# A fused retention and gated feed-forward kernel: 256-token blocks, two tokens a partition, and nine equal tiles

## The chip, the cores and the metric

The kernel runs on one core of one Trainium2 chip. A core has five engines with a queue of instructions each: TensorE (PE in the profile; its weight loads are shown apart as PEld), VectorE (DVE), ScalarE (ACT), GpSimd (POOL) and SyncE (SP), which here only issues transfers. An engine runs its own queue in order and waits for others through semaphores. Transfers run on 16 DMA engines. TensorE reads from SBUF and writes PSUM, which has eight banks of 2 KB a partition.

The metric is the device time of one execution in microseconds. Three runs of the kernel before gave 299.54, 298.88 and 304.79 us, median 299.54.

## What is computed

The reference has two parts. The first is a retention layer: attention without softmax, with a decay by head. The second is a feed-forward layer with `h * cos(h)` between two matrix products.

```python
def _attn_ref(q, k, v):                    # each (8, 8, 576, 64): batch, heads, tokens, head size
    scale = 1.0 / np.sqrt(D_)
    scores = scale * np.matmul(q, k.transpose(0, 1, 3, 2))
    gamma = 1.0 - 2.0 ** (-5.0 - np.arange(H))
    rel = pos[:, None] - pos[None, :]
    Dmat = np.where(rel >= 0, gamma[:, None, None] ** rel[None, :, :], 0.0)
    return np.matmul(scores * Dmat, v)

def _moe_ref(x, w_in, w_out):              # x (4608, 512), w_in (512, 2048), w_out (2048, 512)
    h = x @ w_in
    g = h * np.cos(h)
    return g @ w_out
```

The attention's output, with the heads side by side, is `x`: 8 x 576 = 4608 rows of 512. Inputs and output are float32.

## The kernel before

**Attention.** The 4608 tokens are taken in 36 groups of 128. A batch entry has 576 tokens, that is four and a half groups, so every ninth group is mixed: its second half begins a new entry. For one group:

- `load` (L105) fetches q, k and v, tokens on partitions, with one piece of 64 floats (256 bytes) for each token and head. It is issued from SP.
- `prep` (L131) multiplies q and k by powers of the head's decay (`scaled`, L139) and rounds to bf16, and rounds v. This is on POOL, 1.05 us for q, 1.05 to 1.14 us for k and 0.65 us for v. The powers (`gq`, `gk`) are made at the start from token positions.
- `transposes` (L163) turns q and k so that the head size lies on partitions: on TensorE for groups 0 to 5, and from group 6 by a transposing DMA from SP (L166).
- `scores` (L186) makes k times q for the eight heads, and VectorE multiplies the result by a triangular mask (L206).
- `state` (L218) and `states` (L247) keep the sum of k times v over the tokens of the entry so far. VectorE adds (L286), and a copy in bf16 follows (L277).
- `attn_out` (L292) adds the masked scores times v (`own`, L332) and q times the state (`carried`, L318), and ScalarE or VectorE copies the sum to `xT` (L349).

**Feed-forward.** Rows are taken in tiles; the widths are `[512, 256, 256] + [512] * 7`. `mm1` (L353) makes `h` in blocks of 1024 columns of a two-bank PSUM tile, ScalarE takes the cosine (L372), and VectorE multiplies (L373, `gT`). The first three tiles (rows 0 to 1023) use `mm2` (L375): 16 matmuls of 512 columns for each 128 rows. The other seven tiles use `mm2_seven` (L505), a form of Strassen's method: the product of two 2 x 2 block matrices is made from seven block products (`product`, L467) instead of eight, of 16 matmuls with 256 columns each. It needs sums of quarters of `gT` (`g_sum`, L420; `gs7` is on POOL, the others on VectorE), sums of quarters of `w_out` (`w_sums`, L403) and sums of the results (L515, VectorE).

**Order.** The kernel writes out the order of each engine's queue by hand. The matmuls of the attention of later rows are put between those of the feed-forward of earlier rows: at positions in the lists `todo` for the first tiles, and ahead of some of the seven products (`at`, L820 to L829) for the others. `feed` (L577) is called at each store and issues the next loads, preps and transposes. PSUM banks are named by tags: `a`, `b` and `m` are pairs of banks, `n` and `st` single ones. A new use of a tag waits until the last use has been read out.

**Start.** The first 512 queries come with four tokens a partition (L620), keys and values group by group. TensorE runs 14 matmuls on zeros while they come (L641). The weights come in eight transfers of a quarter of a matrix, cast to bf16, issued from POOL between the first preps; the load of group 4 waits for the sixth of them (L704).

Of the kernel before, what the change touches and what calls it, by code (L numbers as in the profile page):

```python
# [8 lines left out]
F32 = mybir.dt.float32  # L9
# [8 lines left out]
def kernel(  # L18
# [9 lines left out]

# [4 lines left out]
    HG = H // 2  # L39
    DM, DF = moe_w_in.shape  # L40
# [3 lines left out]
    NG = NTOK // P  # L44
    PER = 2 * S // P
    MIX = PER // 2
    HP = P // 2
# [3 lines left out]
    ET = DF // P  # L51

    widths = [512, 256, 256] + [512] * 7
    assert sum(widths) == NTOK
    starts = [sum(widths[:n]) for n in range(len(widths))]
    N_PE_T = 6
    S7 = 3
    LD = 5

    consts = ctx.enter_context(tc.tile_pool(name="consts", bufs=1))  # L60
    first = ctx.enter_context(tc.tile_pool(name="first", bufs=1))
    ld = ctx.enter_context(tc.tile_pool(name="ld", bufs=LD))
    nat = ctx.enter_context(tc.tile_pool(name="nat", bufs=8))
    trp = ctx.enter_context(tc.tile_pool(name="trp", bufs=8))
    retp = ctx.enter_context(tc.tile_pool(name="retp", bufs=4))
# [4 lines left out]
    op = ctx.enter_context(tc.tile_pool(name="op", bufs=2))  # L70
    xp = ctx.enter_context(tc.tile_pool(name="xp", bufs=2))

# [4 lines left out]

    pos_i = consts.tile([P, PER, H], I32)
    pos = consts.tile([P, PER, H], F32)
    lng = consts.tile([P, H], F32)  # L80
    gq = consts.tile([P, PER, H], F32)
    pos_i4 = consts.tile([P, 4, H], I32)
    pos4 = consts.tile([P, 4, H], F32)
    gq4 = consts.tile([P, 4, H], F32)
    gk = consts.tile([P, PER, H], F32)
    ln_scale = consts.tile([P, 1], F32)
    half_pi = consts.tile([P, 1], F32)
    tri = consts.tile([P, P], F32)
    tri_mix = consts.tile([P, P], F32)
    diag2 = consts.tile([P, P], F32)  # L90
    ident = consts.tile([P, P], BF16)
    zeros = consts.tile([P, 512], BF16)
    w_in_sb = consts.tile([P, DG, DF], BF16)
    w_out_sb = consts.tile([P, ET, DM], BF16)

    v_odd = consts.tile([P, 2, H, D], BF16)

    blocks4 = [consts.tile([P, HG, D], BF16, tag=f"sb{x}", name=f"sb{x}") for x in range(4)]

    tiles = {}  # L100
# [4 lines left out]
    def load(g, names="qkv", gate=None):  # L105

        t0 = g * P
        if g % PER == MIX:
            parts = [(0, HP, t0), (HP, P, t0 + HP)]
        else:  # L110
            parts = [(0, P, t0)]
        for name in names:
            src = {"q": q, "k": k, "v": v}[name]
            f = ld.tile([P, H, D], F32, tag="f" + name, name=f"f{name}")
            for p0, p1, t in parts:
                b, s0 = divmod(t, S)
                i = nc.sync.dma_start(  # L117
                    f[p0:p1], src[b, :, s0 : s0 + p1 - p0, :].rearrange("h s d -> s h d")
                )
                if gate is not None:  # L120
                    tc.add_manual_dep(
                        i.ins, gate.ins.name,
                        mybir.DependencyInfo(
                            mybir.DependencyClass.Sync, mybir.DependencyReason.DATA
                        ),
                        reason="weights first",
                    )
                    gate = None
            tiles["f" + name, g] = f

    def prep(g, early=False, kv_first=False):  # L131

        c = g % PER
        fk, fv = (tiles.pop(("f" + n, g)) for n in "kv")
        qks = nat.tile([P, 2, H, D], BF16, tag="qks", name="qks")
        vb = nat.tile([P, H, D], BF16, tag="vb", name="vb")
        qkT = trp.tile([P, 2 * HG, P], BF16, tag="qkT", name="qkT")

        def scaled(eng, m, f, by):  # L139
            eng.tensor_tensor(  # L140
# [8 lines left out]
        if not early and not kv_first:  # L149
            scaled(nc.gpsimd, 0, tiles.pop(("fq", g)), gq)  # L150
# [724 lines left out]
```

## Time and profile before

The profiled execution took 298.52 us, of which 296.8 lie between the first and the last instruction (the span).

| what | value |
|---|---|
| median of three runs, us | 299.54 |
| profiled execution, us | 298.52 |
| its span, us | 296.8 |
| first block of `h` starts, us | 17.95 |
| `h` without a break from, us | 19.73 |
| last addition on VectorE ends; last store issued; span ends, us | 293.35; 294.4; 296.8 |
| DMA bytes | 50.29 MB in 154305 packets |

The largest groups of instructions, as `line engine operation, shape and count | busy us, mean ns | idle time of the engine before them and what ended it`:

```profile
L373 DVE TENSOR_TENSOR gT<-h,cosh 128x1024 bf16<-128x1024 f32 x72 | 88.0, 1222 | 36.4 <-ACT cosh L372 36.3
L372 ACT ACTIVATE cosh<-h,half_pi 128x1024 f32<-128x1024 f32 x72 | 80.2, 1113 | 66.7 <-PE h L364 66.7
L140 POOL TENSOR_TENSOR qks<-fq,gq 128x512 bf16<-128x512 f32 x32 | 33.6, 1052 | 60.8 <-DMA fq<-in_q_dram 56.4
L206 DVE TENSOR_TENSOR ret<-sc,tri 128x1024 bf16<-128x1024 f32 x32 | 38.1, 1218 | 2.8 <-PE sc L194 2.7
```

In the chain of waits, which is followed back from the last instruction, TensorE has 80% of the span, DMA 8% and VectorE 6%. The mean duration of a matmul in the groups is longer than the distance from one start to the next, since matmuls overlap in the array; prices of matmuls are therefore read from a run of them, its length over its count. POOL's line 140 is idle for 56.4 us in all until its query loads arrive; the engine's idle time is no loss where nobody waits for it.

### The profile page before, as it was taken

What the parts mean: (1) busy time and instruction counts of PE and PEld (TensorE: products, weight loads), DVE (VectorE), ACT (ScalarE), POOL (GpSimd) and SP (SyncE); (2) the same over time, 40 slices, a digit from 0 to 9 for tenths busy, and PEclk for the clock granted to TensorE, in tenths of its full rate; (3) what the DMA queues carried; (4) which work ended last, traced back from release to release, by engine and by line L of the source; (5) the groups of instructions that cost most, each with busy time, mean ns of one, the idle gap of its engine ahead of it and who ended that gap; (6) DMA issues with size and microseconds to landing.
All of it is one profiled execution on the core that took longest, in us unless ns stands there. A gap on an engine that the chain in (4) does not pass through costs nothing.

```text
span 296.8 us, 7293 instructions
## 1 busy us (share of the span) xinstructions
PE 285.0 (96%) x3083; PEld 195.9 (66%) x3105; DVE 215.4 (73%) x265; ACT 133.9 (45%) x163; POOL 133.7 (45%) x147
## 2 busy tenths in 40 slices
PE   8899999999999999999999899999999999999994
PEld 3478646858568886457745685488448844884584
DVE  5677718564668996797969856996699669935943
ACT  2656432605246534652456344644464346425620
POOL 2750056445444484683675962389139013101410
PEclk9999999999999999999999999999999999999999
DMA  8999999999999999999999999998950340111013
GB/s 205 213 208 207 211 200 209 201 228 219 220 177 213 203 234 215 208 286 167 185 205 243 231 202 225 198 219 214 225 95 5 95 120 0 38 59 49 0 38 107
DMA packets 154305, 50.29 MB, mean 169 GB/s; under 512 B 140832, under 2 KB 153248, under 8 KB 154272
## 3 DMA queue, kind: packets, MB, share of 16 engines
q1 hardware_dynamic: 149504, 45.10, 77.6%
q0 software_dynamic: 4224, 4.19, 8.5%
q8 instruction: 24, 0.39, 0.6%
q10 hardware_dynamic: 544, 0.52, 0.5%
q14 instruction: 9, 0.07, 0.1%
HBM read 36.70 MB, written 9.44 MB: 155 GB/s over the span
## 4 chain that ended last, share of the span: by engine, by line
PE 80%; DMA 8%; DVE 6%; SPq 2%; issue 1%; ACT 1%; POOL 0%; DVEq 0%
PE h L364 39%; PE o L495 26%; PE o L381 7%; DMA qkT<-qks 4%; DMA fk<-in_k_dram 2%; DMA w_in_sb<-in_moe_w_in_dram 2%; PE sc L194 2%; PE ov L332 2%; DVE gT L373 2%; PE ov L318 2%; DVE gs L437 1%; SPq L117 1%; PE st L265 1%; DVE ot L515 1%; DVE ret L206 1%
## 5 line engine op out<-in xcount | busy, mean ns | idle before, releaser
L364 PE MATMUL h<-xT,w_in_sb 128*128 128x512 bf16 (+2 forms) x820 | 126.8, 313 | 1.5 <-DVE xT L349 0.7
L373 DVE TENSOR_TENSOR gT<-h,cosh 128x1024 bf16<-128x1024 f32 x72 | 88.0, 1222 | 36.4 <-ACT cosh L372 36.3
L372 ACT ACTIVATE cosh<-h,half_pi 128x1024 f32<-128x1024 f32 x72 | 80.2, 1113 | 66.7 <-PE h L364 66.7
L364 PEld LDWEIGHTS <-w_in_sb 128*128 128x128 bf16 x832 | 75.9, 98 | 49.9 <-issue 1.0
L437 POOL TENSOR_TENSOR gs<-gT 128x512 bf16<-128x512 bf16 x24 | 30.6, 1282 | 69.0 <-DVE gT L373 69.0
L140 POOL TENSOR_TENSOR qks<-fq,gq 128x512 bf16<-128x512 f32 x32 | 33.6, 1052 | 60.8 <-DMA fq<-in_q_dram 56.4
L495 PEld LDWEIGHTS <-gs 128*128 128x128 bf16 x456 | 43.1, 98 | 5.8
L140 POOL TENSOR_TENSOR qks<-fk,gk 128x512 bf16<-128x512 f32 x35 | 39.8, 1138 | 9.4 <-DMA fk<-in_k_dram 8.3
L206 DVE TENSOR_TENSOR ret<-sc,tri 128x1024 bf16<-128x1024 f32 x32 | 38.1, 1218 | 2.8 <-PE sc L194 2.7
L495 PEld LDWEIGHTS <-gT 128*128 128x128 bf16 x336 | 32.4, 98 | 6.5 <-DVE gT L373 1.1
L519 ACT COPY ot<-o 128x512 f32<-128x512 f32 x28 | 16.4, 585 | 43.2 <-PE o L495 43.2
L515 DVE TENSOR_TENSOR ot<-ot,o 128x512 f32<-128x512 f32 x34 | 22.6, 683 | 11.9 <-ACT ot L519 7.9
L381 PE MATMUL o<-w_out_sb,gT 128*128 128x512 bf16 x120 | 28.9, 380 | 0.5 <-issue 0.2
L495 PE MATMUL o<-w_out_sb,gT 128*128 128x256 bf16 x224 | 26.6, 273 | 0.6 <-DVE gT L373 0.5
L495 PE MATMUL o<-ws,gs 128*128 128x256 bf16 x224 | 26.8, 273 | 0.0
L495 PE MATMUL o<-w_out_sb,gs 128*128 128x256 bf16 (+1 forms) x232 | 26.8, 269 | 0.0
L155 POOL CAST vb<-fv 128x512 bf16<-128x512 f32 x32 | 20.9, 652 | 8.6 <-DMA fv<-in_v_dram 8.0
L349 ACT CAST xT<-ov 128x1024 bf16<-128x1024 f32 (+1 forms) x18 | 16.5, 917 | 14.2 <-PE ov L318 12.1
L381 PEld LDWEIGHTS <-gT 128*128 128x128 bf16 x128 | 11.8, 98 | 12.5
L437 DVE TENSOR_TENSOR gs<-gT 128x512 bf16<-128x512 bf16 (+1 forms) x22 | 14.6, 664 | 0.4
L495 PE MATMUL o<-ws,gT 128*128 128x256 bf16 x112 | 13.4, 273 | 0.0
L194 PEld LDWEIGHTS <-qkT 64*64 64x64 bf16 (+1 forms) x512 | 8.9, 105 | 6.5 <-ACT qkT L176 2.3
(69 smaller groups left out, 175.4 us busy)
## 6 DMA issues: line engine op xcount, KB each, us to landing
out_dram<-ot SPq DMA_DIRECT2D x35, 256.0 KB, 3.5
fk<-in_k_dram SPq DMA_DIRECT2D x32, 256.0 KB, 5.0
fv<-in_v_dram SPq DMA_DIRECT2D x32, 256.0 KB, 5.2
fq<-in_q_dram SPq DMA_DIRECT2D x30, 256.0 KB, 4.7
w_in_sb<-in_moe_w_in_dram POOLq DMA_DIRECT2D x4, 512.0 KB, 9.5
w_out_sb<-in_moe_w_out_dram POOLq DMA_DIRECT2D x4, 512.0 KB, 16.7
fq<-in_q_dram SPq DMA_DIRECT2D x8, 128.0 KB, 3.7
fk<-in_k_dram SPq DMA_DIRECT2D x8, 128.0 KB, 4.5
```

Source lines behind the costliest of these rows:

```text
L140: eng.tensor_tensor(out=qks[:, m].rearrange("p (b a) d -> p a b d", a=2), in0=f.rearrange("p (a b) d -> p a b d", a=2), in1=by[:, c, :].re ...
L155: nc.gpsimd.tensor_copy(vb, fv)
L206: nc.vector.tensor_tensor(out=ret.rearrange("p a b i -> p (a b) i"), in0=ps.rearrange("p a b i -> p (a b) i"), in1=mask.unsqueeze(1).to_br ...
L349: evac(tiles["x", n][:, :, t0 : t0 + len(gs) * P], ps.rearrange("p c x i -> p c (x i)"))
L364: nc.tensor.matmul(ps[:, j, :], lhsT=w_in_sb[:, dg, (et + j) * P : (et + j + 1) * P], rhs=xT[:, dg, c0 : c0 + w], start=(dg == 0), stop=(d ...
L372: nc.scalar.activation(cosh, ps, ACTF.Sin, bias=half_pi, scale=1.0)
L373: nc.vector.tensor_mul(gT[:, et : et + m, c0 : c0 + w], ps, cosh)
L381: nc.tensor.matmul(ps, lhsT=gT[:, et, tsi * P : (tsi + 1) * P], rhs=w_out_sb[:, et, :], start=(et == 0), stop=(et == ET - 1),)
L437: eng.tensor_tensor(out=tiles["gs", n, x][:, e : e + step], in0=a[:, e : e + step], in1=b[:, e : e + step], op=op_,)
L495: nc.tensor.matmul(dst[i], lhsT=lhs[:, e, j * P : (j + 1) * P], rhs=rhs[:, e, c0:c1], start=(fresh and e == 0 and (i == 0 or len(parts) > 2)),
L515: return lambda: nc.vector.tensor_tensor(out=out_, in0=in0, in1=in1, op=ALU.add)
L519: nc.scalar.copy(t, tiles["all", x])
```

## The change

The kernel function is written anew around the same arithmetic.

- Tokens come in 18 blocks of 256. Queries have two tokens a partition (pieces of 512 bytes) in all blocks, keys and values in the first four (`NP_B = 4`, "pair" blocks); later keys and values keep 256-byte pieces. A block is two chunks of 128 tokens.
- In a pair block a chunk lies on 64 partitions, two tokens deep (`y`). Scores, states and outputs go over `y`; the outputs of a chunk need twice as many matmuls with half the rows, with a drain of TensorE between two halves of them. The columns of `xT` are now even tokens first, then odd ones, so each store is split in two, one for each half of the partitions (`stored_rows`).
- Blocks 0 to 3 are transposed on TensorE, the others by one transposing DMA per block (twice the columns, half the count).
- There are nine tiles of 512 rows. Tile 0 uses 512-column matmuls, now with all four row groups side by side; the eight others use the seven products. Seven of ten tiles did before.
- The loads of block 2 wait for the fifth weight transfer, and the sixth to eighth are issued on POOL between the scalings of block 2; the loads of block 3 wait for the seventh.
- Scalings and transposes of later blocks are issued by `steps_to` at fixed places: after blocks of `h` in tile 1, then at stores.
- `w_sums(7)` moves to POOL. The result buffers `ot` go from two of each tag to one.

```diff
-    widths = [512, 256, 256] + [512] * 7
+    W = 512
+    NT = NTOK // W
+    BK = 256
+    NP_B = 4
+    AHEAD = 3
...
+    def load(j, names="qkv", gate=None):
+        for name in names:
+            src = {"q": q, "k": k, "v": v}[name]
+            if name == "q" or j < NP_B:
+                f = ld.tile([P, H, 2, D], F32, tag="f" + name, name=f"f{name}")
+                for p0, p1, t in parts_of(j * BK, BK, 2):
+                    b, s0 = divmod(t, S)
+                    i = nc.sync.dma_start(
+                        f[p0:p1].rearrange("p h r d -> p h (r d)"),
+                        src[b, :, s0 : s0 + 2 * (p1 - p0), :].rearrange(
+                            "h (p r) d -> p h (r d)", r=2
+                        ),
+                    )
...
+    def scores_y(j, y, banks):
+        pss = [psum.tile([P, HG, P], F32, tag=t, name="sc") for t in banks]
...
+        for he in range(2):
+            nc.vector.tensor_tensor(
+                out=ret[:, he, :, y, :],
+                in0=pss[he],
+                in1=mask[:, y].unsqueeze(1).to_broadcast([P, HG, P]),
+                op=ALU.mult,
+            )
...
+            for swap in (1, 0):
+                for hg in range(0, HG, 2):
+                    for c in chunks[j]:
+                        he = c.k ^ swap
+                        for y in range(2):
+                            for h in (head(he, hg), head(he, hg + 1)):
+                                one(c, h, y, ret[c.rows, he, h % HG, y, :])
+                if swap:
+                    nc.tensor.drain()
...
+    def stored_rows(r0, c0, c1, t):
+        rows = out[r0 : r0 + P * t.shape[1], c0:c1].rearrange(
+            "(j i r) c -> r i j c", r=2, i=HP
+        )
+        for r in range(2):
+            nc.sync.dma_start(rows[r], t[r * HP : (r + 1) * HP])
...
+    def step():
+        nonlocal prepared
+        if prepared < NB:
+            prep(prepared)
+            transpose_dma(prepared)
+            round_v(prepared)
+            prepared += 1
+            load_next()
...
+    w_dma += [load_w_in(e) for e in (1024, 1536)] + [load_w_out(0)]
...
+    load_next(names="kqv", gate=w_dma[4])
...
+    for name in "kq":
+        for y in range(2):
+            scaled(nc.gpsimd, 2, name, y)
+        w_dma += [load_w_out(4 + "kq".index(name) * 4)]
+    round_v(2)
+    w_dma += [load_w_out(12)]
+    load_next(names="kqv", gate=w_dma[6])
...
+    blocks_of = {
+        0: [(et, h * BK, BK) for et in range(0, ET, 4) for h in range(2)],
+        1: [(et, 0, BK) for et in range(0, ET, 4)] + [(et, BK, BK) for et in (0, 8, 4, 12)],
+    }
...
+    def block2_scores():
+        masks = scores(2, "ab")
+        masks[0]()
+        add = sums_of(2, "a")
+        masks[1]()
+        add()()
...
+                (0, 0): {2: lambda: outputs(1, "a", act, vec)},
+                (1, 1): {1: lambda: scores_y(3, 0, ("n", "st"))},
+                (1, 2): {1: lambda: scores_y(3, 1, ("n", "st"))},
+                (1, 3): {2: block3_sums},
...
+            if (n, i) == (1, 1):
+                steps_to(5)
+            if (n, i) == (1, 3):
+                outputs(3, "b", act, vec)
+                for e in range(0, E2, 2):
+                    w_sums(7, e, e + 2)
+            if (n, i) == (1, 5):
+                steps_to(6)
...
+        if n in (1, 2):
+            at = {6: only_intro, 5: mid_unit, 3: end_unit}
+        else:
+            at = {2: first_unit, 5: second_unit} if n < last else {}
+
+        def stored(u):
+            if n == 1:
+                steps_to({3: 7}.get(u, 0))
+            elif n == 2:
+                steps_to({0: 8, 1: 9, 2: 10, 3: 11}[u])
+            else:
+                steps_to({0: 2 * n + 6, 1: 2 * n + 7}.get(u, 0))
```

In this diff an `intro` is the states and scores of a block with their masks, `outputs` the outputs of a block and their copy to `xT`; `only_intro`, `mid_unit`, `end_unit`, `first_unit` and `second_unit` put one of each ahead of the product that they are listed under. The seven products run in the order 1, 2, 6, 4, 7, 5, 3.

## The prediction

> **What bounds the kernel now.** I read the page's first two parts, then TensorE's timeline, then the chain of waits, and last the timelines of the engines that feed TensorE. From the page:
>
> ```profile
> PE 285.0 (96%) x3083; PEld 195.9 (66%) x3105; DVE 215.4 (73%) x265; ACT 133.9 (45%) x163; POOL 133.7 (45%) x147
> ...
> PEclk9999999999999999999999999999999999999999
> DMA  8999999999999999999999999998950340111013
> ```
>
> The clock is full and TensorE is never idle for a whole slice. The DMA engines are busy until about 222 us, which matters only where TensorE waits for them. Its timeline (start, length, what, idle before it) says how often:
>
> ```profile
> 67.53 7.15 PE L364 MATMUL h<-xT,w_in_sb 128*128 128x256 bf16 x64 [0.69 <-DVE xT L349]
> ...
> 82.80 0.42 PE L194 MATMUL sc<-qkT 64*64 64x128 bf16 x16 [0.53 <-DMA qkT<-qks]
> ...
> 166.60 0.42 PE L194 MATMUL sc<-qkT 64*64 64x128 bf16 x16 [1.34 <-DMA qkT<-qks]
> ```
>
> All such gaps between 19.7 and 292.6 us come to about 4.0 us. So the span is a start-up of 19.7, then 272.9 of nearly unbroken matmuls, then a tail of 4.2. Fewer or faster loads cannot give much by themselves; a change wins by fewer matmul columns or gaps and loses by new gaps. The chain (start, length, count) has the unit prices:
>
> ```profile
> 33.48 9.23 PE o L381 x42
> ...
> 100.20 3.49 PE o L495 x32
> ...
> 179.54 10.74 PE h L364 x49
> ...
> 208.80 10.74 PE h L364 x49
> ...
> 238.24 10.74 PE h L364 x49
> ...
> 267.02 10.74 PE h L364 x49
> ```
>
> A 512-column matmul is 0.22 us, a 256-column one 0.109, one of the seven products (16 of them) 1.75. A late tile takes 29.3 (the starts lie 29.3, 29.4 and 28.8 apart): 13.8 first layer, 12.2 products, 3.3 attention. Attention of 256 tokens is, in TensorE's timeline, 0.37 states, 0.57 scores, 0.9 outputs.
>
> **Matmuls.** Rows 512 to 1023 had 64 second-layer matmuls of 512 columns, 14.1 us; seven products take 12.2: -1.9. Half of their first layer ran in 128-column pieces of 0.060 each (7.6 us), now 64 of 0.109 (7.0): -0.6. Both are on the path. Added on TensorE: transposes of two more groups (+0.9) and, for blocks 2 and 3, twice the state matmuls and a drain each. No row shows a drain; its bounds are 0 and the 0.4 of the longest "issue" gap, I take 0.2, for both blocks with the states +1.0.
>
> **Start-up.** The first loads (3.1 MB) have 512-byte pieces, where keys and values had 256 bytes and the first queries 1024. Two stretches of the windows show what those moved (last number, GB/s):
>
> ```profile
> 4.00:5.00 1.00, 1.00 (x4) 0.30 (x2) 0.17 (x1) 0.00 (x0) 0.00 (x0) 1.00 1.08 378
> 8.00:9.00 1.00, 0.92 (x11) 0.65 (x9) 0.26 (x1) 0.80 (x1) 0.73 (x1) 1.00 1.35 218
> ```
>
> The new size lies between; time per piece interpolated gives 300, so the last of the six (v of block 1) lands at 12.7 us; bounds 10.6 and 16.7. [...] It changes little, because the loads are not what ends last: TensorE's warm-up ends at 6.7 as before; k and q of block 0 are scaled, transposed and copied (VectorE 0.69, ScalarE 0.58 a step) by 9.4; scores at 10.1; two masks in series of 1.22 to 12.5; outputs of block 0 to 13.4, their copies to 15.7. Block 1 repeats it: scores at 16.3, masks at 17.5 and 18.7, state sum 0.69, rounding 0.55, second half of its outputs at 20.3. The first eight first-layer matmuls sit in that wait, as they did before; the same point lay at 19.7. So 20.3, with 18.8 and 22.5 from the bounds of the loads. Iotas, masks and constants (13 iotas of 0.16 on POOL) end by 4, before k has landed; uncovered they would cost 1.
>
> **Tile 0.** 13.1 + 14.1 + attention 4.2 = 31.4. Two waits come in. (a) Block 2's states take bank "a", which VectorE's mask (1.22) has to leave first, while TensorE has no other instruction in its queue: 1.3. (b) The weights. They went out in one run from POOL's queue at 11.0 to 18.7; the last landed at 37.7, 2.8 us apart. Now loads of block 2 wait for the fifth piece (26 us by that pace), and pieces 6 to 8 are issued on POOL behind its scaling of exactly those loads: k lands 4.5 later (30.5), two scalings of 1.05, issue; piece 6 lands 5 to 6.9 later (the first piece took 6.9), about 38. TensorE wants it at 37.3. I take 1, bounds 0 and 4. Tile 0 ends at 54.0.
>
> **Tile 1 (rows 512 to 1023).** First layer 14.0 and block 3's attention 2.4. It is a relay: the second half of block 3's scores needs banks that VectorE's masks of the first half free, and those stand behind the first gT, which stands behind the cosine: 1.75 + 0.2 + 1.11 + 1.23 + 1.4 = 5.7 after the tile's start, TensorE is there at 4.2: 1.5. Then block 3's outputs end 11.5 after the start; their copy on VectorE stands behind a gT, its cosine behind a rounding on ScalarE and that behind the state sum: 9.9 + 0.7 + 0.6 + 1.1 + 1.2 + 0.7 = 14.2. The next first-layer block needs that copy: 2.6, and 0.6 within the outputs. So 21.1. Products 12.2, attention of blocks 4 and 5 3.7, a late mask 0.8: 16.7. Ends at 91.8.
>
> **Tile 2.** 13.8 + 12.2 + 4.6 (three blocks' states and scores, two outputs). A transpose is now one per 256 tokens; those of 128 landed 3.1 to 6.2 after issue (median 4.1), the double one I take at 5, bounds 4 and 8. Block 7 is scaled on POOL only behind this tile's last sum there; in the tile that starts at 148.1 that row is
>
> ```profile
> 163.09 1.27 POOL L437 TENSOR_TENSOR gs<-gT 128x512 bf16<-128x512 bf16 x1 [1.93 <-DVE gT L373]
> ```
>
> 16 us into the tile. Two blocks of 5.7 follow: block 8's transpose can go out 27 after the start, on SP's queue behind the 1.5 MB load of block 10 and two stores, and lands at 33; TensorE is at block 8's scores at 29. With 0.3 for block 7 and a late mask of 0.4: 4.3, bounds 1 and 8. Ends at 126.7.
>
> **The rest.** Tiles 3 to 6 as now, 4 x 29.3 (transposes there are sent some 15 us ahead; uncovered, 4 each); tile 7 28.8; tile 8 25.9. TensorE ends at 298.6. The tail doubles its stores, since each half of the partitions is now a store of its own:
>
> ```profile
> 292.92 1.49 SPq L568 DMA_DIRECT2D out_dram<-ot  x3
> ```
>
> Six issues of 0.5 instead of three: 4.2 + 1.4 = 5.6. [...]
>
> Sum: 298.6 + 5.6 = 304.2 span, and 1.7 outside it (298.52 against 296.8) gives 305.9, against 298.52 for the profiled run, which lies 1.0 below the median of 299.54. Forecast 306, 2.2% over that median; own range 302 to 310.
>
> **Rivals.** First: the waits are covered. If VectorE's relay in tile 1 runs ahead and the transposes land in time, gaps stay at the 4.0 of now instead of my 12.1 (1.3, 1, 4.7, 0.8, 4.3); then 305.9 - 8.1 = 297.8, not slower: the columns saved decide. For it speaks that POOL now waits 56.4 us for query loads, which arrive faster; against it that the relay is of instructions in order, not of loads. It decides if tile 1's products begin by 71 us rather than 75. Second: faster. The same with no gap left at all, and a start-up of 18.8: 305.9 - 12.1 - 1.5 = 292.3. Against it: VectorE is busy for 73% of the span already, and the relays run through it. Third: the weights are late. Each of pieces 6 to 8 needs a load, a scaling and a landing in series; at 4 for each of two pieces instead of 1 in all, 313.
>
> **How the numbers follow.** Forecast 0.50, covered waits 0.26, faster 0.08, late weights 0.16. A measurement of this kernel tells about 2% from no change (the three runs lie that far apart), so "slower" begins at 305.5 and "faster" at 293.5. Of the forecast's range nearly half lies under 305.5 by width, but late weights and unseen waits only add: slower 0.33 of it + 0.16 = 0.49; same 0.17 + 0.21 = 0.38; faster 0.08 + 0.05 of the covered case = 0.13. Range 296 to 314: from the covered case to just past the late weights.
>
> **What would show it.** Right: a wait of the first layer on the copy of block 3's outputs of 2 to 3 us near 66; a wait of scores on qkT near 121; six late stores. Wrong: tile 1's products before 71; first-layer matmuls unbroken before 18.5; w_out waits over 4 us near 37 (third rival).

## The result, and the profile after

The changed kernel takes 315.1 us (median of 4 runs, 314.74 to 316.29) against 299.57 for the kernel before on the same chip: a ratio of 1.0533, with a 95% interval of 1.0494 to 1.0573. The forecast was 306 with a range of 296 to 314. Slower was right; the loss is 15.5 us where 6.5 were forecast. Some executions run in a second state (of the kernel before, on one chip, 303.68 us at a mean clock of 0.991 beside 299.28 at 0.998); the ratios and the experiments' times leave these out, so a ratio can differ a little from that of two medians.

The profiled run took 315.27, with a span of 313.6. First the top of its page: busy time by engine, then the two rows of the forty slices that differ most from before.

```profile
PE 288.6 (92%) x3258; PEld 197.4 (63%) x3258; DVE 220.1 (70%) x270; ACT 136.3 (43%) x158; POOL 152.6 (49%) x182
...
PEclk9799999998999999589999999999999999999997
DMA  7996989999998829999999819964700530121014
```

The row of TensorE's clock was all nines before. Now it has a 7 in the second slice, an 8 in the tenth and a 5 and an 8 near 130 us: the clock was halved for part of these slices (0.50 and 0.51 in the windows below). (The last 7 lies behind the last matmul.) The DMA engines now have slices with room, which before came only after 222 us.

TensorE's timeline has the waits, each with its releaser in brackets. Its columns are start, length, line and what, idle time before.

```profile
25.46 10.64 PE L457 MATMUL h<-xT,w_in_sb 128*128 128x256 bf16 x96 [1.65 <-DVE gT L466]
...
44.55 0.81 PE L331 MATMUL st<-v_mix,qks 64*64 64x64 bf16 x32 [1.37 <-DVE ret L247]
...
68.22 0.38 PE L457 MATMUL h<-xT,w_in_sb 128*128 128x256 bf16 x2 [1.13 <-ACT xT L444]
69.60 6.63 PE L457 MATMUL h<-xT,w_in_sb 128*128 128x256 bf16 x44 [1.00 <-DVE xT L445]
...
123.80 0.41 PE L387 MATMUL ov<-ret,vb 128*64 128x128 bf16 x8 [1.43 <-DVE ret L277]
124.15 0.42 PE L419 MATMUL ov<-qkT,sb 64*64 64x128 bf16 x16
129.08 1.07 PE L267 MATMUL sc<-qkT 64*64 64x128 bf16 x32 [4.51 <-DMA qkT<-qks]
130.08 3.60 PE L557 MATMUL o<-w_out_sb,gs 128*128 128x256 bf16 x16
```

The longest is 4.51 us, for the transpose of block 8. The last row shows what follows: 16 matmuls of one product take 3.60 us, where those from 119.99, at full clock, take 1.92.

SP's queue shows why that transpose is late (here a length includes the time until SP could go on):

```profile
117.26 0.59 SPq L134 DMA_DIRECT2D fq<-in_q_dram  x1
117.90 1.70 SPq L148 DMA_DIRECT2D fk<-in_k_dram  x2
119.70 2.61 SPq L148 DMA_DIRECT2D fv<-in_v_dram  x2
122.41 2.64 SPq L573 DMA_DIRECT2D out_dram<-ot  x2
125.16 1.80 SPq L196 DMA_TRANSPOSE qkT<-qks  x1
```

POOL had scaled block 8 by 120.87. The transpose went out at 125.16, behind a load and two stores, and landed at 129.08.

The windows give the granted clock by stretch: after the stretch, PE busy, PEld, DVE, ACT, POOL (each with a count), clock, DMA share, GB/s.

```profile
67.00:70.00 3.00, 0.87 (x14) 0.65 (x7) 1.82 (x2) 1.17 (x2) 3.00 (x4) 1.00 0.86 193
70.40:73.70 3.30, 3.30 (x18) 2.32 (x16) 0.31 (x1) 1.11 (x1) 1.17 (x3) 0.51 1.04 255
...
121.50:124.90 3.40, 1.64 (x44) 1.05 (x42) 2.70 (x4) 0.28 (x1) 3.40 (x4) 0.99 1.14 255
124.90:135.00 10.10, 5.92 (x52) 3.85 (x53) 3.09 (x4) 1.03 (x2) 7.32 (x10) 0.50 0.95 225
```

Both stretches at half clock follow one in which TensorE was busy for half of the time or less (0.87 us of 3.00, 1.64 of 3.40). The price is half of the busy time there: 1.65 us of 3.30, and 2.96 of 5.92. In windows of 0.1 us the half clock lasts from 70.25 to 73.66 and from 124.86 to 135.10, that is 3.41 and 10.24. A third such stretch lies in the start, from 12.22 to 15.63, behind three microseconds in which TensorE was busy for 1.65. The three begin 17 and 16 times 3.41 us apart, so in this run they lie on a grid of 3.41 us.

Here the steps of the forecast stand beside the trace (us from the span's start; a tile is counted from its first layer to that of the next):

| | forecast | changed kernel | before |
|---|---|---|---|
| first layer unbroken | 20.3 | 21.0 | 19.7 |
| tile 0 ends | 54.0 | 55.6 | |
| rows 0 to 1023 end | 91.8 | 94.5 | 84.7 |
| tile 2 takes | 34.9 | 39.0 | 31.6 |
| tiles 3 to 8 take | 171.9 | 173.2 | 176.5 |
| tail | 5.6 | 6.9 | 4.0 |

### The profile page after: what moved, and what is told of

The parts are those of the page before. It is cut to its first block, busy times and chain, and to the rows that moved or that the text cites. A ratio compares the mean times of both kernels' runs of the same rounds, so it can differ in the third digit from the quotient of the medians.

```text
span 313.6 us, 7653 instructions
## 1 busy us (share of the span) xinstructions
PE 288.6 (92%) x3258; PEld 197.4 (63%) x3258; DVE 220.1 (70%) x270; ACT 136.3 (43%) x158; POOL 152.6 (49%) x182
## 3 DMA queue, kind: packets, MB, share of 16 engines
q1 hardware_dynamic: 124672, 45.10, 60.5%
## 4 chain that ended last, share of the span: by engine, by line
PE 70%; DMA 9%; POOL 8%; DVE 5%; issue 3%; ACT 1%; SPq 1%; DVEq 0%; POOLq 0%; ACTq 0%
PE h L457 33%; PE o L557 28%; POOL qks L165 4%; DMA w_out_sb<-in_moe_w_out_dram 4%; DMA fk<-in_k_dram 3%; PE o L865 3%; DVE gT L466 2%; DMA fv<-in_v_dram 2%; PE ov L387 2%; PE sc L267 2%; PE st L331 1%; ACT cosh L465 1%; POOL vb L176 1%; DMA qkT<-qks 1%; PE ov L419 1%
## 5 line engine op out<-in xcount | busy, mean ns | idle before, releaser
L457 PE MATMUL h<-xT,w_in_sb 128*128 128x512 bf16 (+1 forms) x704 | 129.8, 345 | 3.8 <-DVE gT L466 1.6
L457 PEld LDWEIGHTS <-w_in_sb 128*128 128x128 bf16 x704 | 69.6, 99 | 60.4 <-issue 5.2
L557 PEld LDWEIGHTS <-gs 128*128 128x128 bf16 x520 | 50.2, 99 | 7.3 <-issue 0.2
L557 PEld LDWEIGHTS <-gT 128*128 128x128 bf16 x384 | 37.1, 98 | 6.2
L277 DVE TENSOR_TENSOR ret<-sc,mask_c 128x1024 bf16<-128x1024 f32 x25 | 29.8, 1213 | 4.8 <-PE sc L267 4.8
L165 POOL TENSOR_TENSOR qks<-fk,gkc 128x512 bf16<-128x512 f32 x28 | 31.3, 1137 | 0.0
L557 PE MATMUL o<-ws,gs 128*128 128x256 bf16 x256 | 30.7, 273 | 0.0
L176 POOL CAST vb<-fv 128x512 bf16<-128x512 f32 x36 | 22.5, 653 | 1.4 <-DMA fv<-in_v_dram 1.4
L442 ACT CAST xT<-ov 128x1024 bf16<-128x1024 f32 x14 | 14.2, 1012 | 12.2 <-PE ov L419 12.2
L371 ACT CAST sb<-s 128x512 bf16<-128x512 f32 (+1 forms) x18 | 10.3, 574 | 18.2 <-DVE s L359 7.7
L387 PE MATMUL ov<-ret,vb 128*64 128x128 bf16 (+1 forms) x352 | 12.9, 229 | 3.9 <-DVE ret L277 1.9
L361 DVE TENSOR_TENSOR s<-st,s 128x256 f32<-128x256 f32 x18 | 7.6, 423 | 11.7 <-PE st L331 11.4
L504 DVE TENSOR_TENSOR gs<-gT 128x512 bf16<-128x512 bf16 (+1 forms) x25 | 15.4, 615 | 0.4
```

Of the source, the lines that this page charges most:

```text
L165: return eng.tensor_tensor(out=dst.rearrange("p b a d -> p a b d"), in0=src.rearrange("p (a b) d -> p a b d", a=2), in1=by.rearrange("p (a ...
L176: runs[y](vb[:, y], f[:, :, y, :] if j < NP_B else f[:, y])
L277: nc.vector.tensor_tensor(out=ret[:, k].rearrange("p a b i -> p (a b) i"), in0=pss[k].rearrange("p a b i -> p (a b) i"), in1=mask.unsqueez ...
L387: nc.tensor.matmul(ps[h % 2 * D : h % 2 * D + D, h // 2, c.c0 : c.c0 + P], lhsT=vb[c.rows, y, h, :], rhs=rhs, start=part not in begun, sto ...
L442: evac(x, ps)
L457: nc.tensor.matmul(ps[:, j, :], lhsT=w_in_sb[:, dg, (et + j) * P : (et + j + 1) * P], rhs=xT[:, dg, c0 : c0 + w], start=(dg == 0), stop=(d ...
```

## The experiments

Each edit is made to the changed kernel, and each was timed against the kernel before on its chip. As the chips' times for the kernel before differ a little (medians 298.8 to 299.5), ratios are compared: 1.0533 is the changed kernel, and 0.01 is 3.0 us.

### The late transpose, and the clock behind it

**One store earlier.**

```
-                steps_to({3: 7}.get(u, 0))
+                steps_to({1: 7, 3: 8}.get(u, 0))
-                steps_to({0: 8, 1: 9, 2: 10, 3: 11}[u])
+                steps_to({0: 9, 1: 10, 2: 11, 3: 11}[u])
```

> Tile 2's two late scalings and transposes (blocks 7 and 8) are sent one store earlier; nothing else is moved. Theory A (the 4.5 us wait of block 8's scores is the transpose's place in the queues, and the half clock from 125 to 135 us follows from that wait): the wait goes, and about 3 us of half-speed matmuls after it go too, so the span falls by 7 to 8, to about 306. Rival B (a transpose of 256 tokens is slow in itself): the wait stays within 1 us, span over 312. Rival C (the low clock has another cause): only the wait goes, span about 309.

309.21 us, ratio 1.0328 (1.0279 to 1.0377): 6 us less, where theory A said 7 to 8. TensorE's timeline of this kernel at the same place:

```profile
127.47 0.41 PE L387 MATMUL ov<-ret,vb 128*64 128x128 bf16 x8 [1.43 <-DVE ret L277]
127.82 0.42 PE L419 MATMUL ov<-qkT,sb 64*64 64x128 bf16 x16
128.06 0.62 PE L267 MATMUL sc<-qkT 64*64 64x128 bf16 x32
128.61 1.92 PE L557 MATMUL o<-w_out_sb,gs 128*128 128x256 bf16 x16
```

The scores follow without a wait, they take 0.62 instead of 1.07, the product 1.92 instead of 3.60, and tile 2 takes 32.5 instead of 39.0. The wait and the clock behind it are worth more than the wait alone. In this kernel's profiled run, tile 1 waited 1.74 and 2.72 us for the transposes of blocks 4 and 5, which the changed kernel's profiled run did not: those two are marginal as well. With them tile 1 took 42.7 us instead of 38.9, and the clock was halved from 91.4 to 94.8 instead of at 70.

**Zeros in the pause.** To part the wait from the clock, 20 matmuls on zeros stand ahead of block 8's scores.

```
-        masks = scores(j, sc_banks)
+        masks = scores(j, sc_banks, idle=idle)
...
-                intro(b + 1, "ba", "a", pend, then)
+                intro(b + 1, "ba", "a", pend, then, idle=20)
```

> Twenty matmuls on zeros (about 4.3 us) are put ahead of block 8's scores, in the bank that the scores use next; the wait itself is left as it is. Theory A (TensorE's idleness lowers the granted clock): the clock stays at 1.0 from 125 to 135 us, the scores start at about the same time, and what follows runs at full speed: span 3 lower, about 310.5. Rival C (the clock falls for another reason): half clock stays, span 313 or more.

314.2 us, ratio 1.0529 (1.0453 to 1.0605). In its trace the clock stays full (1.00 in each microsecond from 124 to 140):

```profile
125.12 4.49 PE L218 MATMUL sc<-zeros 128*128 128x512 bf16 x19
130.19 0.64 PE L267 MATMUL sc<-qkT 64*64 64x128 bf16 x32 [0.57 <-DMA qkT<-qks]
130.76 1.92 PE L557 MATMUL o<-w_out_sb,gs 128*128 128x256 bf16 x16
```

Scores and product run at full speed; tile 2 takes 37.9 (39.0), and the first layer of tile 3 13.8 (14.6). The half clock near 12 and near 70 us, where nothing was filled, is still there. So the halved clock behind the pause is shown as an effect of TensorE's idleness, with about 2 us in the trace. The time did not fall by the 3 us that theory A said; the ratio did not move, and its interval is too wide to say more.

### The tail

**One store over 128 partitions, with the rows of a block left in split order** (this leaves out the interleaving of even and odd rows in the result).

```
-        rows = out[r0 : r0 + P * t.shape[1], c0:c1].rearrange(
-            "(j i r) c -> r i j c", r=2, i=HP
-        )
-        for r in range(2):
-            nc.sync.dma_start(rows[r], t[r * HP : (r + 1) * HP])
+        rows = out[r0 : r0 + P * t.shape[1], c0:c1].rearrange("(j p) c -> p j c", p=P)
+        nc.sync.dma_start(rows, t)
```

> Every store is one transfer of 128 partitions instead of two of 64; the result rows come out in the wrong order, which leaves out the interleaving of even and odd rows and nothing else. If the split costs its issue time on SP's queue: the tail from the last matmul falls from 7.0 to about 4.5, and block 8's transpose, which stands behind two stores, goes out about 1.3 earlier, so its wait falls by about 1: span 309.5 to 311. Rival (the two halves move in parallel and the tail is the landing of the last bytes): tail within 0.5 of 7.0, span over 312.5.

311.05 us, ratio 1.0402 (1.0376 to 1.0429): 3.9 us less, of which the tail is 3.0 (3.97 instead of 6.94). SP's queue at the end, first of the changed kernel, then of this one:

```profile
298.72 12.24 SPq L573 DMA_DIRECT2D out_dram<-ot  x12
```

```profile
297.39 9.48 SPq L570 DMA_DIRECT2D out_dram<-ot  x6
```

These lengths hold the waits for the sums too. In the changed kernel the issue of a half store takes 0.55 to 0.60 us there, and the last ten go out back to back, 6.44 us long, so the queue lags behind the sums; here the issue of a whole store takes 0.35 to 0.50 (at the end of the kernel before 0.34 to 0.58, median 0.38). The edit also does away with the writing of every second row, so which of the two makes the issue of a half longer is not shown. Part of the rest is tile 1 (37.9 instead of 38.9 us), where the same pause did not halve the clock. Windows of this kernel:

```profile
67.00:70.50 3.50, 1.19 (x36) 0.76 (x29) 1.82 (x2) 1.94 (x3) 3.50 (x5) 1.00 0.89 210
70.50:74.00 3.50, 3.50 (x34) 3.13 (x33) 0.70 (x1) 1.27 (x2) 2.53 (x4) 1.00 0.98 237
```

TensorE was nearly as idle here (1.19 of 3.50 busy) as in the changed kernel. What differs is how the pause lies on the grid of 3.41 us on which the half-clock stretches of these two runs begin (here at 13.59 and 126.22, 33 times 3.41 apart): in the changed kernel one stretch of the grid, 66.84 to 70.25, holds nearly all of it (1.28 of 3.41 busy), here two share it (2.78 and 1.63, from 64.80 and from 68.21). So a pause of nearly the same length was followed by half clock in one run (0.51) and by full clock in the other (1.00); that its place on the grid decides is read from these two and not tested by itself.

**Rows put in order at the copy.** The copy of the outputs to `xT` writes them in the order of the rows, and the store is the one above, so nothing is left out.

```
...
+            x.rearrange("p g (c i r) -> p g c r i", r=2, i=HP),
+            ps.rearrange("p g (c r i) -> p g c r i", r=2, i=HP),
```

> The rows are put back in order at the copy of the attention outputs (it writes every second column), so each store is one transfer over 128 partitions with right rows. Theory (split stores cost the tail 3 us, nothing else): the tail is 4.0 instead of 6.9 and the time 312.1, as with the stores joined and rows left out of order (311.1). Rival: strided writes make the copies slower (now 1.1 us for a whole block), and TensorE waits for xT in tile 1 and elsewhere: tail 4.0, but the time 314 or more and the wait for the copy in tile 1 over 3 us.

313.12 us, ratio 1.0444 (1.0345 to 1.0544). The tail is 3.96. The copies became slower (0.73 instead of 0.59 for half a block on ScalarE, 1.31 instead of 1.01 for a whole one), and TensorE waits 0.61 and 0.38 for the first of them. From 23.1 to 26.5 us the clock is halved as well, and the wait of 1.65 at 25.5 falls away in that; tile 0 takes 39.2 instead of 38.0 us, from its first matmul on. So part of the 3 us is given back at the start.

### The relay of tile 1

**Block 3's outputs copied by ScalarE alone**, and its state rounded by VectorE.

```
-        sums_of(3, "n")()()
+        sums_of(3, "n")()(vec)
...
-                outputs(3, "b", act, vec)
+                outputs(3, "b", act)
```

> Block 3's state is rounded on VectorE instead of ScalarE, and its outputs are copied by ScalarE alone, so that the cosine of tile 1's fourth block does not stand behind the rounding and the copy does not stand behind a gT on VectorE. Theory (relay): the first-layer block that waits for the copy starts 1.0 to 1.8 earlier (69.6 now), and if the pause of TensorE gets short enough the half clock at 70.4 to 73.7 goes as well, another 1.7: span 310 to 312.5. Rival (the wait belongs to the DVE queue as a whole): the start moves by less than 0.5, span 313 or more.

316.57 us, ratio 1.0596 (1.0531 to 1.0661): nothing gained. TensorE's timeline:

```profile
68.79 7.15 PE L457 MATMUL h<-xT,w_in_sb 128*128 128x256 bf16 x64 [1.11 <-ACT xT L442]
80.23 0.32 PE L331 MATMUL st<-vb,qks 128*64 128x64 bf16 x8 [0.80 <-DVE gT L466]
81.84 0.77 PE L267 MATMUL sc<-qkT 64*64 64x128 bf16 x32 [1.29 <-DMA qkT<-qks]
```

The relay was relieved as forecast: the first layer of tile 1 takes 19.5 instead of 22.5 us. TensorE then comes sooner to block 4's scores, whose transpose has not landed, and the clock is halved from 82.2 to 85.6. The products take 20.3 instead of 16.5. The gain is turned into a new wait.

**Transposes ahead of loads.** Both edits above (one store earlier, the relay), and the transposes of blocks 4 and 5 ahead of the loads of 6 and 7.

```
-            load_next()
+            steps_to(5)
...
-            if (n, i) == (1, 1):
-                steps_to(5)
...
+                steps_to(6)
             if (n, i) == (1, 5):
-                steps_to(6)
+                load_next()
```

> Three edits at once: the transposes from block 6 on one store earlier (as in the first experiment), block 3's outputs copied by ScalarE alone (as in the fourth), and the transposes of blocks 4 and 5 sent ahead of the loads of blocks 6 and 7. Theory: the fourth experiment gained 2.9 us in tile 1's first layer and lost it at once to block 4's transpose, which stood behind two loads on SP's queue; with it ahead of them the gain stays: tile 1 takes 36 to 37 instead of 39, tile 2 32.5 instead of 39, the time is 305 (304 to 307). Rival: the transfers themselves are what is slow there (the DMA engines are busy until 80 us), so a transpose ahead of the loads lands no sooner or makes the loads late: a wait for qkT of over 1 us stays in tile 1, and the time is 309 as with the first edit alone.

312.04 us, ratio 1.0407 (1.0341 to 1.0473). Tile 1 takes 36.1 as the theory said (56.1 to 92.2), but tile 2 35.0, and tile 3 34.2 instead of 29.4. There TensorE waits 3.18 us for ScalarE's copy of a product, which waits for a store that SP sent late. Block 8's scores in tile 2 wait 1.20 for their transpose, and behind each of the two waits 3.4 us run at half clock (from 123.7 and from 154.4), which costs 1.7 each. What is moved ahead on the queue of loads, transposes and stores pushes something else back.

### The sine table, and a surprise

**An early sine.** A dummy sine loads ScalarE's table in idle time (the load takes 1.28 us at 21.74, in front of the first cosine).

```
+    sine = consts.tile([P, 1], F32)
+    nc.scalar.activation(sine, half_pi, ACTF.Sin, bias=half_pi, scale=0.0)
```

> One dummy sine on ScalarE before the first scores, so that the 1.28 us table load at 21.74 us is done before the first cosine needs it. Theory: that load makes the first gT late, and with it the wait of 1.65 us of the first layer at 25.5 us; the wait shrinks to about 0.4 and the time is 313.8, 1.3 under the changed kernel's 315.1. Rival: the wait comes from the order of the banks (the third block of the first layer takes bank m again, right behind cosine and product of the first one), and the table load only fills idle time of ScalarE: the wait stays over 1.2 and the time at 315.

329.19 us, ratio 1.0955 (1.0842 to 1.1068): 13 us worse. The wait at 25.5 us did shrink as the theory said, from 1.65 to 0.71. What got worse is the transfers. Here is the main queue's row of the page (packets, MB, share of 16 engines' span), first of the changed kernel, then of this one:

```profile
q1 hardware_dynamic: 124672, 45.10, 60.5%
```

```profile
q1 hardware_dynamic: 124672, 45.10, 70.0%
```

The same packets and bytes take a fifth more time (70.0% of a span of 328.4 against 60.5% of 313.6). The new tile of 4 bytes moved the tiles behind it in the memory. With it all six edits above were put together:

> All together: the earlier transposes, block 3's copy on ScalarE, blocks 4 and 5 ahead of the loads, rows in order with one store, the sine table early, and 20 matmuls on zeros ahead of block 8's scores. If the terms add (305, less 2.9 for the tail and 1.3 for the table): 301, with a range of 299 to 303, which is within 1% of the kernel before, and the granted clock is 1.00 from 20 us on. If they do not add, because some pause of TensorE of over 2 us is left and halves the clock, or because the order only moves a wait: 305 or more, with a half-clock stretch in the profile.

319.0 us, ratio 1.0640 (1.0532 to 1.0748), q1 at 69.2%. It told nothing about the sum, as its addresses were moved too.

**Addresses alone.** An unused tile of 32 bytes, in the changed kernel and in the kernel before, and in the changed kernel one of 128 bytes:

```
+    space = consts.tile([P, 8], F32)
+    nc.gpsimd.memset(space, 0.0)
```

> The changed kernel with 32 bytes of unused constants a partition in front, so that every tile filled by a transfer begins 32 bytes past a multiple of 64 (the compiled program gives fq 84768 for 84736) and nothing else differs. Theory (address): the run with the dummy sine lost 14 us because its 4-byte tile moved all later tiles so, not because of the sine; this kernel takes 326 to 331 as well, q1's packets take 69 to 70% of 16 engines' span instead of 60.5%, with the same packets and bytes. Rival (sine): the ScalarE table was to blame, or chance in the chip: 315 and 60 to 61%.

> The kernel before with 32 bytes of unused constants a partition, which puts its tiles on multiples of 64 (fq from 90592 to 90624); before they lay 32 bytes past. Theory (address): its transfers get faster too, q1's share falls from 77.6% to 65 to 70%; TensorE waits for transfers only 2 to 3 us there, so the time falls by 1 to 3 us, to about 298. Then the change itself owes something to its address: against the shifted kernel before it is 6% slower rather than 5%. Rival: pieces of 256 bytes do not mind the address, or their packets have slack: 77% and 300 as before.

> The changed kernel with 128 bytes of unused constants in front (fq at 84864 for 84736). Theory (the step is 128 bytes): as the changed kernel, 315, q1 at 60 to 61%. Rival (the step is 256 bytes or more): as with 32 bytes, 326 to 332 and 69 to 70%.

Two runs of edits together, with the sine in a tile of 64 bytes, belong to the same question:

> Three edits that each gained where they were made: transposes from block 6 on one store earlier (-6), rows in order and one store (-2.9 in the tail), and the early sine, now in a tile of 64 bytes so that addresses stay on multiples of 64 (-1.0: the first layer's wait at 25.5 us from 1.65 to 0.7). If they add: 305 (303 to 307). Rival: a pause of TensorE that was hidden behind the removed ones takes their place, or the clock halves elsewhere: 309 or more.

> The kernel with everything, again with the tile of 64 bytes: the three edits and block 3's copy on ScalarE, transposes of blocks 4 and 5 ahead of the loads, 20 matmuls on zeros ahead of block 8's scores. Theory (address): the 319 of the same kernel with the 4-byte tile came from its addresses; now 303 (301 to 306), as the edits add. Rival (one queue): stores, loads and transposes share SP's queue, which is never empty from 40 to 150 us, so what is moved ahead pushes something else late (in the seventh experiment a store, and by it ScalarE's copy, at 150 us): no better than the three edits alone, 305 or more.

| kernel | where `fq` begins, past a multiple of 256 | GB/s from 4 to 10 us | q1's share | us | ratio |
|---|---|---|---|---|---|
| changed | 0 | 347 | 60.5% | 315.1 | 1.0533 |
| changed, 32 bytes on | 32 | 294 | 69.3% | 331.91 | 1.1094 (1.1037 to 1.1152) |
| three edits, 64 bytes on | 64 | 296 | 69.1% | 317.94 | 1.0646 (1.0615 to 1.0677) |
| all edits, 64 bytes on | 64 | 294 | 67.1% | 318.28 | 1.0641 (1.0569 to 1.0714) |
| changed, 128 bytes on | 128 | 296 | 69.2% | 325.13 | 1.0865 (1.0794 to 1.0936) |
| before | 224 | 263 | 77.6% | 299.5 | 1 |
| before, 32 bytes on | 0 | 299 | 69.1% | 298.6 | 1.0004 (0.9963 to 1.0046) |

The rates are read from windows; here is the changed kernel, then the one with 32 bytes:

```profile
4.00:10.00 6.00, 5.21 (x81) 2.77 (x80) 3.37 (x6) 1.83 (x4) 5.21 (x11) 1.00 1.15 347
```

```profile
4.00:10.00 6.00, 5.21 (x32) 2.09 (x33) 3.10 (x5) 1.86 (x4) 4.51 (x11) 1.00 1.16 294
```

The sine is cleared (the kernel with the early sine has 294 GB/s, as the one with unused bytes), and the address is shown: 32 unused bytes cost the changed kernel 17 us. An offset of 32, 64 or 128 bytes costs the same rate (294 to 296 GB/s), so the step is none of these; 256 fits both kernels, though no run moves the changed kernel by 256. The tile of 64 bytes did not help, and the theory that 128 would was wrong too. With the tiles 64 bytes on, all edits are no better than three of them. The kernel before also transfers faster when it is moved to a multiple of 256 (299 GB/s for 263), but gains no time: TensorE waits for transfers only 2 us there. What moved for the loads in these runs is the place that they write. Which part of a transfer pays is not shown.

TensorE's waits in the changed kernel that was moved by 32 bytes (total, times, longest) show where the time goes:

```profile
PE sc L269 <- DMA qkT<-qks: 12.5, 4, 5.4
PE o L559 <- ACT ot L589: 3.7, 1, 3.7
```

Four transposes are late instead of one, and a copy waits for a store.

### All together, addresses as in the changed kernel

The dummy sine now writes into a tile that is free by then (`kpos`). Three edits (one store earlier, rows in order with one store, early sine):

> Three edits with every address as in the changed kernel (the dummy sine now writes into a tile that is free by then): transposes from block 6 on one store earlier, rows in order with one store, the early sine. Theory (the terms add, and the run of the same three with a tile of 64 bytes lost by its addresses alone): 305 (303 to 307), q1 at 59 to 61%. Rival (they do not add): 309 or more at 59 to 61%, with a wait or a half-clock stretch that the changed kernel had not.

307.46 us, ratio 1.0274 (1.0254 to 1.0294), q1 at 60.1%. Against 317.94 for the same three with the tiles 64 bytes on, 11 us by the ratios are the address alone. Against the changed kernel it is 7.7 us less, 2 short of the 10 that theory said, and between the theory's range and the rival's. Half clock is left from 12 to 19 and near 70 to 74 us.

With the relay's edit and the transposes of blocks 4 and 5 ahead of loads as well, run twice, the second time beside the last kernel of this section:

> The three edits and block 3's copy on ScalarE and the transposes of blocks 4 and 5 ahead of the loads, addresses as in the changed kernel. Theory (what is moved ahead on the one queue pushes something else late): tile 1 takes 36 as in the seventh experiment, and tile 2 or 3 gives it back: 305 to 309, no better than the three edits. Rival (the seventh experiment lost by chance of the clock): 302.

> The version with five edits once more, beside the one with the zeros: 307, with half clock near 12 to 18 and 70 to 73 us, both theories.

307.11 us, ratio 1.0249 (1.0215 to 1.0284), and 305.98, ratio 1.0225 (1.0184 to 1.0265). The number is the theory's, the place is not: tile 1 takes 38.9, so the relay's gain is not there to be given back. The slower copy of block 3 (1.30 us) and the half clock behind it take it, and tiles 2 and 3 take 32.5 and 29.4.

All stores from ScalarE's queue instead of SP's:

```
-        nc.sync.dma_start(rows, t)
+        nc.scalar.dma_start(rows, t)
```

> As the one with all edits, but every store goes out from ScalarE's queue, so that SP's has loads and transposes alone. Theory (the one queue): no store stands behind a load and no transpose behind a store; tiles 2 and 3 take 32.5 and 29.4, and the time is 301 to 303. Rival (the transfers themselves, or ScalarE): a store on ScalarE waits in order for VectorE's sum, the cosines behind it are late: the first layers of tiles 2 to 7 take over 14.5 instead of 13.8, and the time is 309 or more.

319.38 us, ratio 1.0675 (1.0657 to 1.0694). ScalarE's timeline in tile 1:

```profile
58.85 3.23 ACTq L576 DMA_DIRECT2D out_dram<-ot  x2
62.13 0.58 ACT L878 COPY ot<-o 128x512 f32<-128x512 f32 x1 [4.44 <-DMA fk<-in_k_dram]
65.26 2.07 ACTq L576 DMA_DIRECT2D out_dram<-ot  x2
67.38 2.12 ACT L471 ACTIVATE cosh<-h,half_pi 128x1024 f32<-128x1024 f32 x2 [4.67 <-DMA fv<-in_v_dram]
```

The issue of a store holds ScalarE for 1 to 1.6 us here (two take 3.23, the next two 2.07), and the first cosines of the tile stand behind it. The first layer of tile 1 takes 31 us. The rival is right in the time, and only in part in the place: of the later tiles, 4 and 5 have first layers of 15.5 and 15.4 us, the others 13.8. In this kernel stores are worse off in ScalarE's order than in SP's (319.38 us for 307.11). The theory of the one queue is not refuted by it, since this kernel loses for another reason.

Last, zeros in the three pauses that were left, in the kernel with the five edits:

```
+    warm(psum.tile([P, 512], F32, tag="n", name="idle"), 4)
     transpose_pe(1, "k", "n", act, (0,))
+    warm(psum.tile([P, 512], F32, tag="m", name="idle"), 3)
...
+            if (n, i) == (1, 4):
+                warm(psum.tile([P, 512], F32, tag="m", name="idle"), 6)
```

> The version with five edits, and 13 matmuls on zeros in pauses of TensorE: 4 ahead of the transposes of block 1's k, 3 ahead of block 0's outputs, 6 ahead of the first-layer block that waits for block 3's copy. Theory (the gate answers to idle time within a stretch of some 3.4 us, not to single long gaps): no slice below full clock from 9 us on, the first layer starts unbroken 0.5 to 1 sooner, tile 1 loses 1.7 less, the time is 2 to 3 us under that of the version without (304.5). Rival (the zeros only move the wait, since the copies and masks that TensorE waits for come when they come): the clock full, the time within 1 us of the version without.

305.06 us, ratio 1.0202 (1.0174 to 1.0229). The clock of its page:

```profile
PEclk9999999999999999999999999999999999999999
```

It is full throughout, as theory said, and the first layer of tile 1 takes 20.1 instead of 21.7, the 1.7 of half the stretch. The start gains nothing: the first layer is unbroken from 22.9 with zeros and from 23.0 without, so half clock there lay beside other waits. The profiled spans differ by 2.3 us, as theory said, but the medians by 0.9 with intervals that overlap, so by the time the rival's "within 1 us" holds.

This is the fastest version of the new skeleton, and it is still slower than the kernel before. Rows 0 to 1023 end at 93.0 us in it, at 84.7 before; tile 2 loses 0.9 more (32.5 for 31.6), and tiles 3 and 4 win back 3.7 us (29.7 and 29.4 for 31.9 and 31.0), where the kernel before has waits, the longest 1.34 for a transpose.

## Why the prediction was wrong

**The clock.** "The clock is full" was read from the profile before and carried over to a kernel with other pauses. No step priced what a pause does to the matmuls behind it. In the changed kernel that is 1.65 us in tile 1 and 2.96 at the end of tile 2 and in tile 3, 4.6 in all, half of the 9.4 by which the span was missed (313.6 against 304.2). Zeros in the pauses and the earlier transpose both take the half clock behind these waits away. This sum is the trace's; as a gain in time it is not shown, since zeros alone moved the medians by less than their intervals. The third stretch, from 12.2 us, does not count: filling it let the first layer begin no sooner. What decides when the clock falls is not shown. Its half lasted 3.41, 3.41 and 10.24 us in this trace, and gaps of 1.0 and 1.1 us within three us in which TensorE was busy for 29% were enough for it at 70 us. No busy share separates the cases: TensorE was busy for 55% of the 3 us from 9 to 12, and the clock fell at 12.2; in the kernel moved by 32 bytes it was busy for 45% and 46% of two stretches of 3.41 us (from 194.83), and the clock stayed full.

**The tail.** The split stores were priced at 1.4 us from issues of 0.5 each. They cost 3.0: with one store for each part the tail is 3.97 instead of 6.94. The mechanism was right, the term was mis-sized. A half store takes longer to issue (0.55 to 0.60 us) than a whole one (0.35 to 0.50), where the forecast had 0.5 for either, and the halves queue up: the last ten go out back to back. The tail before is 4.0 in the trace, not the 4.2 that the sum began with.

**Tile 2.** Block 8's transpose behind the load and two stores was named, and its scores waited. The forecast gave all waits 4.3; they are 4.51 and 1.43, the second for a mask given as 0.4. The landing took 3.9 us, not 5, but it was issued 30.7 after the tile's start rather than 27: the stores in front wait for VectorE's sums, 2.0 us. These 1.6 more of waits and 2.2 of half clock within the tile make 3.8 of the 4.1 that tile 2 was missed by. With the transpose one store earlier the wait of 4.51 and the half clock are gone.

**Tile 0 and the start.** The wait for the mask in bank "a" was right: 1.37 for 1.3. The weights' 1 us did not come: no matmul waited for `w_out_sb`, so the third rival falls at these addresses (in the run with the early sine, with the tiles moved, the same wait was 3.40). Missed was the 1.65 at 25.5, of which 0.9 is ScalarE's table load in front of the first cosine. The loads ran at 347 GB/s where 300 was interpolated from the trace before; the kernel before has its tiles 224 bytes past a multiple of 256, and with the tiles moved the changed kernel's rate is 294 to 296, near the 300. That the changed kernel's tiles begin on a multiple of 256 is luck that no step of the prediction looked at: at the other addresses tried it takes 10 to 17 us more, and the miss would have been far larger.

**Tile 1.** The relay was right in kind: waits of 1.13 and 1.00 on the two halves of block 3's copy near 68. The first layer takes 22.5 us, or 20.8 without the half clock, against 21.1. That this sum came so near is partly luck: all waits within it come to 3.1 us (with 0.48, 0.35 and 0.18 before the copy) where 4.7 were forecast, and the rest to 17.7 where 16.4 were. The products took 16.5 against 16.7.

**Matmuls and late tiles.** Tiles 4 to 8 take 29.4, 29.3, 29.4, 28.7 and 26.2, within 0.3 of the forecast; tile 3's 30.2 has 0.8 of half clock in it.

**The rivals.** Covered waits and the faster case both fall: tile 1's products began at 78, not 71. The forecast's direction stands on the relays and the late transpose, and those are there.

Why the gain of fewer matmul columns did not show: it is 2.5 us by the prediction's own count, with 1.9 of added attention work against it, and rows 0 to 1023 end 9.8 us later than before, 8.3 in the best version. There 3.2 of the 8.3 are there when the first layer goes on without a break (22.9 us for 19.7). What of them could be had by another order of VectorE's work was not tried.

## What to carry to other kernels

Price a pause of TensorE twice: its length, and half of the busy time of a half-clock stretch behind it. In the changed kernel the second price was 1.65 us near 70 us, behind three us in which TensorE was busy for 0.87, and 2.96 from 124.9 on, behind 3.40 us in which it was busy for 1.64. Give it a chance, not a certainty: with one store for both halves 1.19 of 3.50 us busy near 70 us cost no clock. Before comparing two versions, look at where tiles begin that transfers fill: here 32 unused bytes moved all of them off a multiple of 256, and that cost 17 us, where the earlier transpose won 6. When work moves ahead on a queue that also carries loads and stores, name what it pushes back.

## What the runs showed of the hardware

- From 4 to 10 us the transfers of 512-byte pieces ran at 347 GB/s into tiles on a multiple of 256 bytes, and at 294 to 296 with the tiles 32, 64 or 128 bytes past it; those of the kernel before ran at 299 on a multiple and at 263 with the tiles 224 bytes past it.
- A transpose of 256 tokens landed in 4.0 us (median of 14), no later than one of 128 (4.1).
- In the changed kernel half clock came in two stretches of 3.41 us and one of 10.24, the last from the pause of 4.51 us on, and they began 17 and 16 times 3.41 us apart; with one store over 128 partitions it began at 13.59 and 126.22, 33 times 3.41 apart.
- One store over 128 partitions instead of two over 64, each of every second row, shortened the tail by 3.0 us, and writing every second column made ScalarE's copy of 128x1024 take 1.31 instead of 1.01 us.
